# First batch of an agent-attention kernel: weights loaded between the key blocks, a later maximum, two results in one PSUM tile

## The chip, the cores and the metric

The kernel runs on one core of a Trainium2 chip. The metric is the device time of one execution in microseconds (us). Five engines work beside each other, each in its own order: TensorE (PE; its weight loads are PEld), VectorE (DVE), ScalarE (ACT), GpSimd (POOL) and SyncE (SP), which here issues every DMA.

## The reference

```python
B, N, C = (4, 12480, 128); n_agents = 49; d_ff = 2048
scale = 1.0 / np.sqrt(C)
def sm(a, b):
    s = scale * (a @ b.transpose(0, 2, 1))
    s = s - s.max(-1, keepdims=True)
    e = np.exp(s)
    return e / (e.sum(-1, keepdims=True) + 1e-09)
agent_v = sm(agents, k) @ v
x = (sm(q, agents) @ agent_v).reshape(B * N, C)
h = np.maximum(x @ w_in, 0.0)
return h * h @ w_out
```

`w_in` (128x2048) and `w_out` (2048x128) come as float64; the kernel decodes their two 32-bit words itself.

## The kernel before

**Two stages.** The first batch's attention over the keys is an opening of its own, some 80 us long, in which nothing else runs. Then a main loop goes over 52 query blocks of 960 tokens in 416 double steps; in it the other three batches' attention is spread between the products of the feed-forward network. The change touches the opening and what directly follows it.

**The opening** is written under `tc.manual_schedule()`: every engine takes its instructions in the order in which the code is written.

- `load_keys`, `load_values`: 13 key blocks (960 keys, 480 KB each) and 14 value blocks (516 KB) go through SP's queue into the tiles `ahead`, `PRE` buffers in rotation. A value block can be loaded once the block that held its buffer has been used. `load_w_in`, `load_w_out` load each weight matrix in four parts of 512 KB (tiles `raw`).
- `key(i)`: 8 matmuls give the scores of a key block for 49 agents in a PSUM bank that `bank()` hands out; ACT copies them to `s`; DVE takes a running maximum, `mx` for blocks 0 to 6 and `mx_late` for 7 to 12.
- `maximum(h)`: DVE reduces the running maximum (`m`), PE transposes it, DVE reduces again and makes a diagonal `dg`, PE spreads it over the partitions, DVE copies that to `mb`. `early` is the first half's, `late` the second's.
- `weigh(i)`: DVE subtracts the maximum, ACT takes the exponential. `gather(i)`: 8 matmuls add the weighted values of block i into PSUM (`psa` for blocks 0 to 6, `o` for 7 to 12).
- `decode_w_in`, `decode_w_out`: for each part one ACT and five DVE operations (`magnitudes`, `remainders`); for `w_in` also the sum and a maximum, for `w_out` a maximum. `powers_of_w_out` makes a power of two of the maxima (one small PE product of `e_out`), `parts_of_w_out` cuts each part into `wo_hi`, `wo_half` and `wo_lo`.
- `queries(0)`: the first query block: scores, exponential `e`, its normalisation on POOL, the split `pp`, two transposing products of `pp` on PE (below: the pp products), and small DMAs.
- `tables(0)`: the gathered sum `x` is multiplied into `w_in` in four chunks of 512 columns. `rl` is the scaled reciprocal; from it on, each chunk gets `aw_hi` (ACT), `aw_lo` and `aw_half` (DVE), and five small DMAs (`aw_hi`, `aw_ex`) that the main loop's products of that chunk wait for.

**The main loop's start.** `first(k)` multiplies a query block with one chunk into two PSUM tiles `h` (two banks each), ACT and DVE square the positive part (`r`, `gg`, `g_hi`, `g_lo`), and four slots later `second(k)` multiplies with `w_out`. Below, the double steps are called step 0, 1, 2 and so on; step 0 to 3 need chunk 0 to 3, and step 2 is the first that is followed by products with `w_out`.

**PSUM.** The pool `ps_h` has three tiles of two banks. In the kernel before, `bank()` takes a new tile for every result of the opening and uses its first bank. A tile is the unit in which the kernel's waits are kept: who writes into a tile waits until those who read what was there before are done.

Of the kernel before, what the change touches and what calls it, by code (L numbers as in the profile page):

```python
# [9 lines left out]
F32 = mybir.dt.float32  # L10
F32R = mybir.dt.float32r
# [16 lines left out]
LAG = 4  # L28
WCH = 512
WARM0 = 16  # L30
PRE = 12
HALF = 7
PAIRED = (0, 2, 4, 6, 1, 3, 5, 7)
PACE = 1.4
ONE = (NT,)
TWO = (NT // 2, NT // 2)
# [13 lines left out]
def agent_attention_relu2(ctx: ExitStack, tc: tile.TileContext, qT, kT, v, agT, w_in, w_out, outT):  # L50
# [81 lines left out]
    def decode_w_in(n, raw):  # L132
        cs = slice(n * WCH, (n + 1) * WCH)
        made = magnitudes(raw, None)
        next(made)
        t = yield from made
        yield
        low = remainders(raw, t)
        yield
        nc.vector.tensor_add(win[:, cs], t.bitcast(F32), low)  # L140
        nc.vector.reduce_max(top[:, n : n + 1], win[:, cs], axis=AX.X, apply_absolute_value=True)
# [5 lines left out]
    def decode_w_out(n, raw):  # L147
        high = raw[:, :, 1]
        nc.vector.reduce_max(most_out[:, n : n + 1], high.bitcast(F32), axis=AX.X, apply_absolute_value=True)
        yield  # L150
        made = magnitudes(raw, high)
        next(made)
        yield from made
        yield
        remainders(raw, high)
# [24 lines left out]
    def parts_of_w_out(n, raw):  # L180
        c = slice(n * WCH // C, (n + 1) * WCH // C)
        up = scale_out[0]
        t, rest = raw[:, :, 1].bitcast(F32), raw[:, :, 0].bitcast(F32)
        hi, lo, half = (x[:, c, :].rearrange("p c d -> p (c d)") for x in (wo_hi, wo_lo, wo_half))
        nc.scalar.activation(hi, t, AF.Copy, scale=up)
        nc.scalar.activation(half, t, AF.Copy, scale=up)
        yield
        nc.scalar.activation(t, t, AF.Copy, scale=up)
        nc.scalar.activation(rest, rest, AF.Copy, scale=up)
        yield  # L190
        nc.gpsimd.tensor_sub(t, t, hi.bitcast(F32))
        last[nc.gpsimd] = nc.gpsimd.tensor_add(lo, t, rest)
# [3 lines left out]

    alone = [True]

    def bank():
        if alone[0]:  # L200
            return ps_h.tile([P, 2, 512], F32, name="h")[:, 0, :]
        return ps_t.tile([P, 512], F32, name="psa", tag=f"turn{1 - turn[0]}")


# [121 lines left out]
    def tables(b):  # L326
        st = state[b]
        qd = quad.rearrange("p h a -> p (h a)")
        x = st.get("x")
        if x is None:  # L330
            x = small.tile([K2, C + 1], F32, name="x")
            nc.vector.tensor_add(x, st["av"][:, : C + 1], st["av"][:, C + 1 :])
            yield 2
        yield -1
        pa = bank()
        put([
            product(pa[:C, :K2], x[:, :C], qd, start=True, stop=True),
            product(pa[:K2, K2 : K2 + 1], qd, x[:, C:], start=True, stop=True),
        ])
        yield 1  # L340
        mag = small.tile([C, K2], F32, name="mag")
        nc.scalar.activation(mag, pa[:C, :K2], AF.Abs)
        av = small.tile([C, K2], F32, name="avT")
        nc.scalar.copy(av, pa[:C, :K2])
        rl = small.tile([K2, 1], F32, name="rl")
        nc.vector.tensor_scalar_add(rl, pa[:K2, K2 : K2 + 1], 1e-9)
        nc.vector.reciprocal(rl, rl)
        if "most" not in state:
            state["most"] = const.tile([C, 1], F32, name="most")
            nc.vector.reduce_max(state["most"], top, axis=AX.X)  # L350
        yield -1
        pu = bank()
        put([product(pu[:K2, :1], mag, state["most"], start=True, stop=True)])
        yield 1
        bound = small.tile([K2, 1], F32, name="bound")
        nc.vector.tensor_mul(bound, pu[:K2, :1], rl)
        yield -1
        ps = bank()
        put([product(ps[:, :1], ones[:K2, :], bound, start=True, stop=True)])
        yield 1  # L360
        size = small.tile([P, 1], F32, name="size")
        nc.vector.tensor_scalar(size, ps[:, :1], 2.0**-30, 2.0**60, op0=ALU.max, op1=ALU.min)
        bits = size.bitcast(U32)
        nc.vector.tensor_single_scalar(bits, bits, 0x7F800000, op=ALU.bitwise_and)
        up = small.tile([P, 1], U32, name="up")
        nc.vector.tensor_scalar(up, bits, -1.0, 280.0 * 2**23, op0=ALU.mult, op1=ALU.add)
        nc.vector.tensor_mul(rl, rl, up[:K2, :].bitcast(F32))
        st["rl"] = rl
        down = small.tile([P, 1], U32, name="down", bufs=2)
        nc.vector.tensor_scalar(down, bits, 2.0, -153.0 * 2**23, op0=ALU.mult, op1=ALU.add)  # L370
        st["down"] = down.bitcast(F32)
        nc.vector.tensor_mul(st["down"], st["down"], scale_out[1])
        hi = st["hi"] = aw.tile([P, FF], F32R, name="aw_hi")
        ex = st["lo"] = aw.tile([P, NCH // NQ, P], F16, name="aw_ex")
        yield 2
        for n in range(FF // 512):
            yield -1
            cs = slice(n * 512, (n + 1) * 512)
            pw = bank()
            put([product(pw[:K2, :], av, win[:, cs], start=True, stop=True)])  # L380
            yield 1
            last[nc.scalar] = nc.scalar.activation(hi[:K2, cs], pw[:K2, :], AF.Copy, scale=rl)
            lo = aw.tile([NA, 512], F32R, name="aw_lo")
            nc.vector.scalar_tensor_tensor(  # L384
                out=lo, in0=pw[:NA, :], scalar=rl[:NA, :], in1=hi[:NA, cs].bitcast(F32),
                op0=ALU.mult, op1=ALU.subtract,
            )
            half = aw.tile([NA, 512], F16, name="aw_half")
            nc.vector.tensor_copy(half, lo.bitcast(F32))
            yield 1  # L390
            nc.sync.dma_start(hi[K2:, cs].bitcast(F32), lo[:SP, :].bitcast(F32))
            for t in range(NQ):
                last[nc.sync] = nc.sync.dma_start(ex[t * 32 : t * 32 + NL, n, :], half[SP:, t * P : (t + 1) * P])  # L393
# [251 lines left out]
    with tc.tile_pool(name="pre", bufs=PRE) as pre, tc.manual_schedule():  # L645
# [2 lines left out]
        q0 = queries(0, pre)  # L648
        for i in range(PRE):
            kts.append(load_keys(0, i, pre, "ahead"))  # L650
            if i in (4, 7, 10):
                ins.append(load_w_in(len(ins)))

        def more(i):
            if i == 0:
                kts.append(load_keys(0, NB - 1, pre, "ahead"))
                next(q0)
                ins.append(load_w_in(len(ins)))
                return
            vts.append(load_values(0, i - 1, pre, "ahead"))  # L660
            nc.gpsimd.memset(vts[-1][:, :, C:], 1.0)
            if i - 1 in (2, 3, 5, 7):
                outs.append(load_w_out(len(outs)))

        mx = [small.tile([TP, NT, NA], F32, name=n) for n in ("mx", "mx_late")]
# [59 lines left out]
        def some(kind, n):  # L725
            if (kind, n) not in begun:
                begun[kind, n] = decode_w_in(n, ins[n]) if kind == "in" else decode_w_out(n, outs[n])
            next(begun[kind, n], None)

        for i in range(NB):  # L730
            key(i)
            more(i)
            if 6 <= i <= 8:
                next(early, None)
            if i == 10:
                weigh(0)
            if i in (3, 4, 5, 7, 8, 9, 10, 11, 12):
                some("in", (i - 3) // 4 if i < 6 else 1 if i < 10 else 2)
        ahead_of(q0, 1)
        more(NB)  # L740
        weigh(1)
        ahead_of(q0, 1)
        next(late)
        powers = powers_of_w_out()
        for i in range(NB):
            if i + 2 < NB:
                weigh(i + 2)
            gather(i)
            if i == 0:
                vts.append(load_values(0, NB - 1, pre, "ahead"))  # L750
                nc.gpsimd.memset(vts[-1][:, :, C:], 1.0)
            if i < 3:
                next(late, None)
                some("in", 3)
            if 1 <= i < NB - 2:
                ahead_of(q0, 1)
            if i == HALF + 1:
                nc.vector.tensor_scalar_mul(x[:NA, :], sums[0][:NA, : C + 1], fall)
            if 3 <= i < NB - 1:
                some("out", (i - 3) // 3)  # L760
            if i == NB - 3:
                some("out", 3)
                next(powers)
            if i == NB - 2:
                run(powers)
        run(q0)
        ahead = queries(1)
        next(ahead)
        cut = [parts_of_w_out(n, outs[n]) for n in range(NW)]
        next(cut[0])  # L770
        next(cut[0])
        spun.append(ps_t.tile([P, 512], F32, name="psa", tag="turn1"))
        spin(2)
        nc.vector.tensor_add(x[:NA, :], x[:NA, :], sums[1][:NA, : C + 1])
        for at, _ in enumerate(tables(0)):
            if at in (1, 3):
                spin(2)
            if at == 2:
                next(cut[1])
        spin(5)  # L780
        seen = small.tile([K2, 1], F32, name="seen")
        nc.gpsimd.tensor_copy(seen, st["rl"])
        run(cut[0])
        some("out", 3)
        some("out", 3)
        for gen in cut[1:]:
            run(gen)
    behind = [last[eng].ins for eng in (nc.sync, nc.scalar, nc.gpsimd)]

# [107 lines left out]
```

## Time and profile before

| | us |
|---|---|
| median of 3 runs (1893.69 to 1894.61) | 1894.58 |
| the profiled execution's own time | 1894.66 |
| its span, first to last instruction | 1892.9 |
| first gather starts | 40.18 |
| first pp product starts | 54.74 |
| `rl` of the tables is scaled, ends | 77.25 |
| step 3 starts, PE without gaps from here | 101.40 |

All times below count from the span's start. The stages follow each other on PE: key blocks, gathers, tables, the first steps of the main loop. From about 101 us to the end PE works without a break that matters, so the length of the opening is read from when PE reaches given instructions. "Granted clock" 1.00 is 2.4 GHz, 0.50 is 1.2 GHz.

### The profile page before, as it was taken

The page shows a single profiled execution, that of the slowest core. Times are in us where ns is not written, and L with a number is a line of the kernel's source. Part 1 is how long each engine was busy: PE and PEld are TensorE (multiplying, and loading weights), DVE is VectorE, ACT ScalarE, POOL GpSimd, SP SyncE. Part 2 cuts the span into 40 slices and gives each one's busy share as a digit, 9 for nine tenths or more (in the row PEclk, how much of TensorE's full clock was granted, in tenths as well). Part 3 has the DMA queues.
Part 4 walks back from the last instruction along what each step waited for, and adds up shares of the span by engine and source line. Part 5 has one row for each costly group of instructions (what it writes and reads, how often), then busy time and mean ns, then how long its engine had stood idle before and what let it go on. Part 6 is the DMA issues. An engine that isn't in the chain of part 4 may idle for free.

```text
span 1892.9 us, 31062 instructions
## 1 busy us (share of the span) xinstructions
PE 1875.7 (99%) x10851; PEld 1426.4 (75%) x10851; DVE 1644.1 (87%) x1870; ACT 1670.0 (88%) x1587; POOL 1326.6 (70%) x1269
## 2 busy tenths in 40 slices
PE   9899999999999999999999999999999999999999
PEld 9677777777777777777777777777777777777776
DVE  5787888888998898888898888888889989899997
ACT  2587899999888899999888889999988999999997
POOL 0255688887666678888766668889866676767675
PEclk7899999999999999999999999999999999999999
DMA  9143222222122222222211212222111111111110
GB/s 366 51 133 105 70 84 95 84 92 83 48 66 71 78 70 83 92 87 90 74 55 60 85 51 66 89 74 75 62 41 56 51 53 52 51 53 44 55 37 28
DMA packets 73780, 145.06 MB, mean 77 GB/s; under 512 B 9244, under 2 KB 45752, under 8 KB 73624
## 3 DMA queue, kind: packets, MB, share of 16 engines
q1 hardware_dynamic: 73624, 143.07, 23.7%
q8 instruction: 86, 1.41, 0.3%
q14 instruction: 70, 0.57, 0.1%
HBM read 83.42 MB, written 25.56 MB: 58 GB/s over the span
## 4 chain that ended last, share of the span: by engine, by line
PE 94%; DVE 3%; ACT 1%; issue 1%; DMA 0%; POOL 0%; SPq 0%; POOLq 0%; ACTq 0%; DVEq 0%
PE o L490 56%; PE h L490 25%; PE psa L490 10%; PE h L674 1%; DVE gg L490 1%; ACT r L490 1%; ACT g_hi L490 0%; DMA ahead<-in_v 0%; PE h L639 0%; PE psa L715 0%; DVE g_lo L490 0%; PE h L224 0%; DVE ob L490 0%; POOL g_lo L521 0%; SPq L393 0%
## 5 line engine op out<-in xcount | busy, mean ns | idle before, releaser
L521 POOL TENSOR_TENSOR g_lo<-gg,g_hi 128x480 f16<-128x480 f32 x832 | 998.3, 1222 | 451.5 <-ACT g_hi L490 256.4
L490 ACT ACTIVATE r<-h 128x960 f32<-128x960 f32 x832 | 763.6, 968 | 125.5 <-PE h L490 98.4
L490 ACT ACTIVATE g_hi<-r 128x1920 fp32r<-128x1920 f32 x416 | 755.0, 1815 | 26.8 <-ACT r L490 0.4
L490 DVE TENSOR_TENSOR g_lo<-h,g_hi 128x960 f16<-128x960 f32 x416 | 480.2, 1154 | 121.3 <-ACT g_hi L490 94.1
L490 PE MATMUL o<-g_hi,wo_hi 128*128 128x480 f32 x1664 | 571.0, 424 | 0.0
L490 DVE TENSOR_TENSOR gg<-r,h 128x960 f32<-128x960 f32 x416 | 478.9, 1151 | 80.6 <-ACT r L490 71.5
L490 PE MATMUL o<-g_lo,wo_half 128*128 128x480 f16 x1664 | 516.6, 370 | 0.7 <-POOL g_lo L521 0.5
L490 PE MATMUL o<-g_hi,wo_lo 128*128 128x480 f32 x1664 | 498.7, 381 | 0.0
L490 DVE TENSOR_TENSOR h<-r,h 128x960 f32<-128x960 f32 x416 | 480.3, 1155 | 0.7
L490 PE MATMUL h<-w,aw_hi 128*128 128x480 f32 x1664 | 433.2, 381 | 5.0 <-DVE aw_lo L384 2.0
L490 PEld LDWEIGHTS h<-w,aw_hi 128*128 128x128 f32 x1664 | 310.3, 188 | 61.1 <-DVE gg L490 8.1
L490 PEld LDWEIGHTS o<-g_hi,wo_hi 128*128 128x128 f32 x1664 | 315.2, 189 | 50.8 <-issue 3.7
L490 PEld LDWEIGHTS o<-g_hi,wo_lo 128*128 128x128 f32 x1664 | 312.7, 188 | 50.5
L490 PEld LDWEIGHTS <-wo_half 128*128 128x128 f16 x1664 | 167.3, 115 | 124.9 <-issue 92.2
L490 PE MATMUL h<-x,aw_ex 19*128 19x480 f16 x1664 | 159.7, 372 | 0.5 <-DMA aw_ex<-aw_half 0.5
L490 PEld LDWEIGHTS psa<-ag,qt 128*120 128x120 f32 x816 | 140.2, 186 | 18.8 <-DVE ob L490 4.4
L490 PE MATMUL psa<-ag,qt 128*120 128x49 f32 x816 | 126.1, 242 | 0.0
L490 PEld LDWEIGHTS <-aw_ex 19*128 19x128 f16 x1664 | 41.9, 91 | 107.3 <-issue 99.9
L490 PEld LDWEIGHTS psa<-ag,kt 128*120 128x120 f32 x624 | 93.5, 184 | 8.6 <-DVE ob L490 0.5
L490 PE MATMUL psa<-ag,kt 128*120 128x49 f32 x624 | 87.6, 249 | 0.0
L307 POOL TENSOR_TENSOR vs<-vt,vs 120x1024 fp32r<-120x1024 f32 x39 | 86.0, 2206 | 0.0
L490 DVE TENSOR_SCALAR ob<-o,down 128x480 f32<-128x480 f32 x104 | 72.4, 696 | 4.0 <-PE o L490 4.0
(165 smaller groups left out, 1046.8 us busy)
## 6 DMA issues: line engine op xcount, KB each, us to landing
qt<-in_qT SPq DMA_DIRECT2D x52, 480.0 KB
out_T<-ob SPq DMA_DIRECT2D x104, 240.0 KB
vt<-in_v SPq DMA_DIRECT2D x39, 516.0 KB
kt<-in_kT SPq DMA_DIRECT2D x39, 480.0 KB
w<-ph SPq DMA_DIRECT2D x102, 91.9 KB
w<-y SPq DMA_DIRECT2D x102, 91.9 KB
x<-half SPq DMA_DIRECT2D x416, 17.8 KB
ahead<-in_v SPq DMA_DIRECT2D x14, 516.0 KB
```

The costliest lines, as they stand in the source:

```text
L307: nc.gpsimd.tensor_sub(vs[:, :, C + 1 : 2 * C + 1], vt[:, :, :C], vs[:, :, :C].bitcast(F32))
L490: ins = issue(*args, **kw)
L521: chain[nc.gpsimd] = nc.gpsimd.tensor_sub(lo[:, n, :], gg[:, n, :], hi[:, 0, n, :].bitcast(F32)).ins
L674: nc.tensor.matmul(sv[:, t, :], kts[i][:, t * TP : (t + 1) * TP], ag[:, 0, :], start=True, stop=True)
```

## The change

- The loads: `PRE` goes from 12 to 11. The four parts of `w_in` are loaded after key blocks 1, 3, 6 and 9, the four of `w_out` after the first four value blocks.
- The decode is spread by two tables: which part takes its next piece after which key block (`BESIDE_KEYS`) and after which gather (`BESIDE_VALUES`). The ACT operation of a part now stands a piece ahead of its DVE operations.
- `early` advances after key blocks 6, 8 and 9 instead of 6, 7 and 8; `weigh(0)` to `weigh(2)` stand behind key blocks 10 to 12.
- `bank()` hands out both banks of a tile, one after the other: two successive results share one tile `h`. In the opening these are key blocks 0 and 1, 2 and 3, 4 and 5, 6 and 7, then block 8 with the transposed maximum, 9 with the spread one, 10 and 11, 12 with the query scores.
- `most`, the maximum of `w_in`, is taken before the gathers. The powers of `w_out` are taken at gathers 6 and 8, and the parts are cut at gathers 9 to 12 and in the tables. Parts 2 and 3 get `wo_lo` from two DVE operations instead of two on ACT and two on POOL.
- `aw_lo` has three buffers and `aw_half` four, instead of two each.

```diff
-PRE = 12
+PRE = 11
+BESIDE_KEYS = ((0, 0), (0, 1), (1,), (1,), (1,), (2, 2), (), (2,), (2, 3), (3,), (3,), (), ())
+BESIDE_VALUES = ((), (), (0,), (1, 0), (2, 0), (3, 0), (1,), (1, 1), (2,), (2, 2), (3,), (3,), ())
...
         nc.scalar.activation(half, t, AF.Copy, scale=up)
         yield
+        if n > 1:
+            for out, x, y, op in ((t, t, hi.bitcast(F32), ALU.subtract), (lo, rest, t, ALU.add)):
+                nc.vector.scalar_tensor_tensor(out=out, in0=x, scalar=up, in1=y, op0=ALU.mult, op1=op)
+            return
...
+    spare = []
+
     def bank():
         if alone[0]:
-            return ps_h.tile([P, 2, 512], F32, name="h")[:, 0, :]
+            if not spare:
+                h = ps_h.tile([P, 2, 512], F32, name="h")
+                spare.extend((h[:, 1, :], h[:, 0, :]))
+            return spare.pop()
...
-            lo = aw.tile([NA, 512], F32R, name="aw_lo")
+            lo = aw.tile([NA, 512], F32R, name="aw_lo", bufs=3)
...
-            half = aw.tile([NA, 512], F16, name="aw_half")
+            half = aw.tile([NA, 512], F16, name="aw_half", bufs=4)
...
-            if i in (4, 7, 10):
+            if i in (1, 3, 6, 9):
                 ins.append(load_w_in(len(ins)))
...
-            if i - 1 in (2, 3, 5, 7):
+            if i - 1 < NW:
                 outs.append(load_w_out(len(outs)))
...
+        some("in", 0)
         for i in range(NB):
             key(i)
             more(i)
-            if 6 <= i <= 8:
+            if i in (6, 8, 9):
                 next(early, None)
-            if i == 10:
-                weigh(0)
-            if i in (3, 4, 5, 7, 8, 9, 10, 11, 12):
-                some("in", (i - 3) // 4 if i < 6 else 1 if i < 10 else 2)
+            for n in BESIDE_KEYS[i]:
+                some("in", n)
+            if i > 9:
+                weigh(i - 10)
...
-            if 3 <= i < NB - 1:
-                some("out", (i - 3) // 3)
-            if i == NB - 3:
-                some("out", 3)
-                next(powers)
-            if i == NB - 2:
-                run(powers)
+            for n in BESIDE_VALUES[i]:
+                some("out", n)
+            if i in (6, 8):
+                next(powers, None)
+            if i == 7:
+                cut = [parts_of_w_out(n, outs[n]) for n in range(NW)]
+            if i > 8:
+                next(cut[(i - 9) // 2])
...
             if at == 2:
-                next(cut[1])
+                next(cut[2])
+            if at == 9:
+                next(cut[3])
+                some("out", 3)
+            if at == 11:
+                run(cut[2])
```

On TensorE, the key blocks of the kernel before, each in a PSUM tile of its own (the number behind `h` is the tile):

```order
L674 MATMUL h_169<-ag_82,ahead_130 120x49 x8
L674 MATMUL h_186<-ag_82,ahead_132 120x49 x8
L674 MATMUL h_201<-ag_82,ahead_134 120x49 x8
L674 MATMUL h_216<-ag_82,ahead_136 120x49 x8
L674 MATMUL h_238<-ag_82,ahead_138 120x49 x8
```

The same place in the changed kernel, on TensorE:

```order
L683 MATMUL h_171<-ag_82,ahead_130 120x49 x8
L683 MATMUL h_171<-ag_82,ahead_132 120x49 x8
L683 MATMUL h_214<-ag_82,ahead_136 120x49 x8
L683 MATMUL h_214<-ag_82,ahead_138 120x49 x8
L683 MATMUL h_253<-ag_82,ahead_142 120x49 x8
L683 MATMUL h_253<-ag_82,ahead_144 120x49 x8
L683 MATMUL h_291<-ag_82,ahead_146 120x49 x8
L683 MATMUL h_291<-ag_82,ahead_150 120x49 x8
L683 MATMUL h_324<-ag_82,ahead_152 120x49 x8
L698 MATMUL h_324<-ident_86,m1_306 49x120
```

Two blocks now stand in one tile, and the built program gives the second of each pair a wait for the readers of the first: block 1 waits for ACT's copy of block 0, blocks 3, 5, 7 and 11 for DVE's maximum of the block before, the transposed maximum for that of block 8, the spread one for that of block 9, and the query scores for that of block 12.

On VectorE, the readers of these tiles in the changed kernel and what stands between them (`t`, `rest`, `raw`, `win` and `top` are the decode of `w_in`):

```order
L691 TENSOR_TENSOR mx_160<-s_180,h_171 120x392
L143 TENSOR_TENSOR win_101<-t_169,raw_134 128x512
L144 TENSOR_REDUCE top_102<-win_101 128x1
L691 TENSOR_TENSOR mx_160<-mx_160,h_214 120x392
L112 TENSOR_SCALAR t_212<-t_212 128x512
L115 TENSOR_SCALAR t_212<-t_212 128x512
L117 SCALAR_TENSOR_TENSOR t_212<-raw_140,t_212 128x512
L691 TENSOR_TENSOR mx_160<-mx_160,h_214 120x392
L124 TENSOR_SCALAR rest_250<-t_212 128x512
L126 SCALAR_TENSOR_TENSOR raw_140<-raw_140,rest_250 128x512
L691 TENSOR_TENSOR mx_160<-mx_160,h_253 120x392
```

The decode of part 0 now stands among the maxima of blocks 1 to 4; in the kernel before it began behind that of block 3.

On VectorE, at the tables, the changed kernel between the first two chunks (`aw_lo_714` and `aw_lo_732`):

```order
L394 SCALAR_TENSOR_TENSOR aw_lo_714<-h_711,rl_688,aw_hi_709 49x512
L399 CAST aw_half_716<-aw_lo_714 49x512
L124 TENSOR_SCALAR rest_720<-raw_268 128x512
L126 SCALAR_TENSOR_TENSOR raw_268<-raw_268,rest_720 128x512
L194 SCALAR_TENSOR_TENSOR raw_248<-raw_248,up_out_609,wo_hi_103 128x512
L194 SCALAR_TENSOR_TENSOR wo_lo_104<-raw_248,up_out_609 128x512
L394 SCALAR_TENSOR_TENSOR aw_lo_732<-h_711,rl_688,aw_hi_709 49x512
```

Four operations on `w_out` have moved in between; before, the second `aw_lo` followed the first `aw_half`.

## Rows read from the trace of the kernel before

**Rows 1.** The page's part 2: granted clock in 40 equal slices, tenths of full speed.

```profile
PEclk7899999999999999999999999999999999999999
```

**Rows 2.** Stretches: length, busy time and count by engine, granted clock, DMA share, GB/s.

```profile
8.00:20.00 12.00, 12.00 (x117) 12.00 (x116) 6.67 (x13) 3.97 (x8) 0.00 (x0) 1.00 1.03 410
23.00:24.00 1.00, 1.00 (x5) 0.83 (x4) 0.70 (x2) 0.45 (x1) 0.00 (x0) 0.50 1.02 408
43.00:44.00 1.00, 1.00 (x7) 0.68 (x6) 0.07 (x1) 0.77 (x2) 0.00 (x0) 0.84 1.06 401
72.00:74.00 2.00, 2.00 (x10) 1.62 (x9) 0.28 (x1) 1.96 (x3) 0.00 (x0) 0.50 0.06 22
84.00:86.00 2.00, 0.28 (x1) 0.00 (x0) 1.34 (x2) 2.00 (x3) 0.53 (x1) 0.57 0.15 37
101.00:102.00 1.00, 1.00 (x5) 0.87 (x4) 0.60 (x4) 0.92 (x1) 0.00 (x1) 0.83 0.76 281
```

**Rows 3.** Timeline of TensorE: start, duration, instruction, count, idle time before and releaser.

```profile
6.93 13.54 PE L674 MATMUL h<-ag,ahead 128*120 128x49 f32 x128
21.28 0.28 PE L689 MATMUL h<-ident,m 120*49 120x120 f32 x1 [0.81 <-DVE m L686]
...
24.01 13.04 PE L674 MATMUL h<-ag,ahead 128*120 128x49 f32 x64
...
40.18 3.48 PE L715 MATMUL psa<-ahead,s 120*49 120x129 f32 x16
...
43.82 1.97 PE L715 MATMUL psa<-ahead,s 120*49 120x129 f32 x16
...
46.06 7.59 PE L715 MATMUL psa<-ahead,s 120*49 120x129 f32 x64
54.74 0.56 PE L224 MATMUL h<-identr,pp 120*98 120x120 f32 x4 [1.09 <-POOL pp L295]
...
61.56 5.52 PE L715 MATMUL o<-ahead,s 120*49 120x129 f32 x48
69.68 0.38 PE L170 MATMUL h<-e_out,ones 128*128 128x1 f32 x2 [2.61 <-DVE e_out L165]
```

**Rows 4.** Timelines of ScalarE and VectorE: a key block's copy and maximum, a decode operation.

```profile
8.75 0.48 ACT L676 COPY s<-h 120x392 f32<-120x392 f32 x1 [6.42 <-PE h L674]
12.62 0.56 DVE L682 TENSOR_TENSOR mx<-mx,h 120x392 f32<-120x392 f32 x1 [1.12 <-ACT s L676]
18.41 0.68 DVE L140 TENSOR_TENSOR win<-t,raw 128x512 f32<-128x512 f32 x1
```

**Rows 5.** The chain of waits, and GpSimd's timeline, ahead of the first pp product.

```profile
45.86 6.15 DMA ahead<-in_v
...
52.27 0.85 POOL e L424
53.74 0.95 POOL L295 TENSOR_TENSOR pp<-e,pp 120x392 fp32r<-120x392 f32 x1 [0.63 <-ACT pp L293]
```

**Rows 6.** Timelines of VectorE and ScalarE: decode of `w_out`, its parts, the tables.

```profile
54.68 0.43 DVE L110 TENSOR_SCALAR t<-t 128x512 f32<-128x512 f32 x1 [2.56 <-ACT t L108]
57.15 0.70 DVE L124 SCALAR_TENSOR_TENSOR raw<-raw,rest 128x512 f32<-128x512 uint32 x1
71.17 0.75 ACT L185 ACTIVATE wo_hi<-raw,up_out 128x512 fp32r<-128x512 f32 x1 [4.55 <-DVE up_out L175]
74.54 0.25 ACT L342 ACTIVATE mag<-h 128x98 f32<-128x98 f32 x1 [0.56 <-PE h L224]
77.09 0.16 DVE L367 TENSOR_TENSOR rl<-rl,up 98x1 f32<-98x1 f32 x1
```

**Rows 7.** Timelines of VectorE and TensorE at the main loop's first steps.

```profile
80.08 0.73 DVE L384 SCALAR_TENSOR_TENSOR aw_lo<-h,rl,aw_hi 49x512 fp32r<-49x512 f32 x1
86.27 2.23 PE L490 MATMUL h<-w,aw_hi 128*128 128x480 f32 x4 [1.99 <-DVE aw_lo L384]
93.69 1.14 PE L490 MATMUL h<-w,aw_hi 128*128 128x480 f32 x2 [1.30 <-issue]
101.40 1.04 PE L490 MATMUL h<-w,aw_hi 128*128 128x480 f32 x4
```

More of the change, by code (lines that the diff above doesn't have):

```diff
@@ L135, in decode_w_in @@
         next(made)
+        yield
         t = yield from made
@@ L152, in decode_w_out @@
         next(made)
+        yield
         yield from made
@@ L347, in tables @@
         nc.vector.reciprocal(rl, rl)
-        if "most" not in state:
-            state["most"] = const.tile([C, 1], F32, name="most")
-            nc.vector.reduce_max(state["most"], top, axis=AX.X)
         yield -1
@@ L655, in more @@
             if i == 0:
-                kts.append(load_keys(0, NB - 1, pre, "ahead"))
+                kts.extend(load_keys(0, n, pre, "ahead") for n in range(PRE, NB))
                 next(q0)
-                ins.append(load_w_in(len(ins)))
                 return
@@ L732, in agent_attention_relu2 @@
             more(i)
-            if 6 <= i <= 8:
+            if i in (6, 8, 9):
                 next(early, None)
-            if i == 10:
-                weigh(0)
-            if i in (3, 4, 5, 7, 8, 9, 10, 11, 12):
-                some("in", (i - 3) // 4 if i < 6 else 1 if i < 10 else 2)
+            for n in BESIDE_KEYS[i]:
+                some("in", n)
+            if i > 9:
+                weigh(i - 10)
         ahead_of(q0, 1)
         more(NB)
-        weigh(1)
+        next(late)
+        some("in", 3)
+        state["most"] = const.tile([C, 1], F32, name="most")
+        nc.vector.reduce_max(state["most"], top, axis=AX.X)
         ahead_of(q0, 1)
-        next(late)
         powers = powers_of_w_out()
         for i in range(NB):
-            if i + 2 < NB:
-                weigh(i + 2)
+            if i + 3 < NB:
+                weigh(i + 3)
             gather(i)
@@ L753, in agent_attention_relu2 @@
                 next(late, None)
-                some("in", 3)
             if 1 <= i < NB - 2:
@@ L768, in agent_attention_relu2 @@
         next(ahead)
-        cut = [parts_of_w_out(n, outs[n]) for n in range(NW)]
-        next(cut[0])
-        next(cut[0])
         spun.append(ps_t.tile([P, 512], F32, name="psa", tag="turn1"))
@@ L782, in agent_attention_relu2 @@
         nc.gpsimd.tensor_copy(seen, st["rl"])
[L783 to L786, printed above, removed]
+        for gen in cut:
             run(gen)
```

## The prediction

> **What bounds the kernel now.** I read the granted clock first. All of the half clock lies in the first two of 40 slices [rows 1], in the opening, and the stretches say where: full speed from 8 to 20 us, half at 23 to 24, back during 43 to 44, half again at 72 to 74, partly at 84 to 86, and full for good during 101 to 102 [rows 2]. So the change, which touches no more than the opening and the first steps, can be priced by when PE reaches four marks: first gather, first pp product, scaled `rl`, step 3.
>
> The timeline of TensorE gives what stands between them [rows 3]. 128 records in 13.54 us are eight key blocks (a matmul has two records, a block 16): 1.69 us each at full clock. 64 in 13.04 are four blocks: 3.26 each at half clock. The blocks follow each other without idle time, since each has its own tile; keys come in at 410 GB/s beside them [rows 2]. So **key phase and gathers are bound by PE and its clock**. The first pp product waits for GpSimd [rows 3], and the chain leads from there to a value load that lands at 45.86 + 6.15 = 52.01 [rows 5]. Later PE waits 2.61 us for `e_out` [rows 3], then the clock is at half [rows 2].
>
> The median, 1894.58, is 0.08 below the profiled execution's 1894.66 with a span of 1892.9; I add differences of marks to 1894.66.
>
> **The change, part by part.**
>
> *First mark, start of the first gather, 40.18 before.* The loads move, but a half-clock PE needs 3.26 us a block where key and weight parts together need some 20 us for all 8.3 MB at 410 GB/s, so they cost nothing while PE is slow. What costs is the shared PSUM tile: the second block of a pair now waits until the first has been read. Block 0 takes no wait; it ends about 8.73 as before, its copy runs from 8.75 for 0.48 [rows 4], and block 1 ends near 11.2, block 2 near 12.9. The copy of block 2 ends near 13.4, VectorE has `win` of the decode ahead (0.68) and then the maximum of 0.56 [rows 4], so block 3 starts near 14.25 and ends near 16.05. A hold is copy 0.48 + maximum 0.56 + three handovers of 0.02 to 0.14, 1.22 together. Such holds stand ahead of blocks 5, 7, 11, of the two products of the early maximum, and of the query scores: six more.
>
> The dear part is what the holds do to the clock. Before, an idle time of 0.81 us ahead of the early maximum's product at 21.28 [rows 3] is followed by half clock at 23 to 24 [rows 2]. Against that, the 1.09 us ahead of 54.74 did not lower it: the gathers behind take 5.52/3 = 1.84 us [rows 3], full speed. One hold may thus pass and a row of them hardly will; I take the fall after the second long hold, at about 16 us. Then ten blocks (4 to 12 and the query scores) at 3.2 are 32.0, six holds 7.3, weight loads that the holds uncover 1.3 (estimate: 0.2 each), the early maximum's two products 0.8: 16.05 + 41.4 = **57.4, +17.2**. Ends: a fall at the first hold, at 11 us, adds 3.0 (two blocks at 1.57 more); a fall only at about 22 us takes 4.7 off; no fall at all gives 41.6 (ten times 1.57 less).
>
> *Second mark, first pp product, 14.56 after the first gather before (54.74 − 40.18).* GpSimd's product `e` waits behind the clearing of the buffer of the last value block's load, and with `PRE` = 11 the last three loads wait for gathers 0, 1 and 2. Three gathers at full speed are 1.9 + 0.16 + 1.97 + 0.27 + 1.9 = 6.2 [rows 3]. The clock returns some way into them: before it took 3.1 us (40.18 to about 43.3, from 0.84 granted at 43 to 44 [rows 2]), a loss of 1.55; at the steps 6.3 us or more (behind 93.69's two products, to about 101.3 [rows 2, 7]), a loss of 3.15; I take 2.4. The load then lies between 1.3 us (516 KB at 401 GB/s [rows 2]) and the 6.15 it took among others [rows 5]; it is the last one in flight, so nearer the lower: 3.3. From landing to pp product it was 2.73: `e` 0.85, `pp` 0.95 and what lies between [rows 5]. Sum 14.6, **+0.1**, first pp product at 72.1. PE's own six gathers take 14.4, no later. Ends: −2.7 (smaller loss 0.8, load 1.9 less) and +3.7 (larger loss 0.8, load 2.9 more).
>
> *Third mark, `rl` scaled, 22.5 later before (77.25).* The 2.61 us wait for `e_out` [rows 3] goes, since the powers are taken at gathers 6 and 8; with it goes the half clock that follows (70.6 to 74, some 1.2 us of work lost; [rows 2] shows 72 to 74), and `most` leaves the chain (0.5, estimate). That would be 18.2. But VectorE and ScalarE now end later. Behind the first pp product VectorE has two decodes of five operations (3 × 0.43 + 2 × 0.70 = 2.7 each [rows 6]), four subtractions of 0.56's size [rows 4] and some eight small ones of 0.16 to 0.43 [rows 6]: +10.0. Then ScalarE: last exponential 0.45, a cast 0.6, `wo_hi` and `wo_half` of part 0 at 0.75 [rows 6], another 0.6, then six full-width operations of 0.68 [rows 4] that stand ahead of `mag` on the two engines: +17.1 for `mag`. From `mag` to scaled `rl` it was 77.25 − 74.54 = 2.7 [rows 6], less `most`'s 0.5: 19.3, **−3.2**. Ends: −4.3 (the waits alone) and −2.0 (two operations of 0.68 more ahead of `mag`).
>
> *Fourth mark, step 3, 24.15 after `rl` before (101.40 − 77.25).* Between the first two `aw_lo` VectorE now has four operations of 128x512, 0.43 + 3 × 0.70 = 2.5 [rows 6]: the second `aw_lo`, which ended at 80.81 = `rl` + 3.56 [rows 7], ends at + 6 to + 7.3, and behind it waits the chunk's DMA, and behind that step 1 (86.27 = + 9.0 before [rows 7]), now about + 12. Step 2 stood at 93.69, + 16.4, with 1.30 idle [rows 7] and VectorE then busy with the rest of a decode, which has gone from there. Step 1's products and query scores, about 5.9 at half clock, put step 2 at + 17.9; to step 3 it is then 7.7 (93.69 to 101.40 at half [rows 7]) or 3.9 at full; with a clock that comes back 3.1 to 6.8 us on, + 23.3 to + 25.6. I take 24.5, **+0.3**; bounds −3.8 (clock never down) and +1.5. Sum: 17.2 + 0.1 − 3.2 + 0.3 = +14.4, **1909**.
>
> **The rivals.**
>
> *A, the clock holds (not slower).* If holds of 1.2 us don't lower the clock, the first gather starts at 41.6; the first pp product is then set by the load, about 54.4 (−0.3); the third and fourth terms stay: −3.2 in all, 1891.5. For it: 1.09 us ahead of 54.74 left the clock up [rows 3]. Against: 0.81 us did not [rows 2, 3], and here six or more follow each other, one every 4.7 us. The point where it decides is the number of blocks at half clock: four of them make it +4.5, one still gives about zero. The Trainium skill, "TensorE: Matmul & The Clock Gate", section "🎯 Why this matters for your kernels", warns of idle gaps between bursts that are longer than any hold here; by that rule the clock would stay and A would hold. The trace does not agree with it: the fall behind the 0.81 us.
>
> *B, the halves don't hold each other.* If the two banks of a tile were independent, keys would end as PE allows: no holds, the key phase at full clock, gathers from about 31.4, but the first pp product still bound by the last value load, at about 54.1 (a little earlier than before, as loads start earlier), then −3.2 + 0.3: 1891.2. Against it: the built program has the waits. The Trainium skill, "PSUM — Partial Sum Buffer", section "🎯 Summary: rules for kernel authors", advises a different bank for reading while a matmul runs; by it the pairs could overlap and B would hold. No run here shows that, and the waits are kept by tile.
>
> *C, the clock falls at the first hold* and returns late in the gathers: +3.0 and +1: 1913.
>
> *D, the clock falls late*, at block 5 to 9: five to eight blocks at half clock, 1.57 each less than the ten: 1899 to 1905.
>
> **How the numbers follow.** Forecast (fall at about 16 us, 1905 to 1911) 0.58; A 0.12; B 0.03; C 0.12; D 0.15. Likeliest 1909. The range takes the forecast, C with its unknown load (to 1914) and D but for its end, from 1900: a little over 0.8. About 0.2%, 3.8 us, is what a measurement here tells from no change: 1890.8 to 1898.4. A and B lie in that, at its lower end; a little more gain in the third mark makes them faster: 0.05 faster, 0.10 within, 0.85 slower.
>
> **What would show it.** In the changed kernel's profile TensorE should have idle times of 1.1 to 1.4 us, released by VectorE's `mx`, ahead of blocks 3, 5, 7, 11 and the query scores; granted clock 0.50 from about 16 to 60 us; four key blocks in 13 us there; first gather at 57 ± 3; first pp product near 72 behind GpSimd's `pp`; no 2.6 us wait for `e_out`; `rl` scaled near 91.5; step 3 near 116, and from there the same rows as before, 14 us later. I am wrong if the blocks between the holds take 1.7 us (A), if there are no holds (B), if the first pp product does not follow the third gather's load (second mark), or if `mag` waits for PE and not for ScalarE (third mark).

## The result, and the profile after

The changed kernel takes 1909.18 us (median, 1907.02 to 1909.75) where the kernel before takes 1894.53, measured beside it: a ratio of 1.0076, interval 1.0059 to 1.0094. It is slower by 14.65 us. The profiled execution is the shortest of the four, 1907.02 with a span of 1905.2; its marks are compared below with those of the profiled execution before.

| mark | before | after | difference of the stretch | predicted |
|---|---|---|---|---|
| first gather starts | 40.18 | 57.02 | +16.84 | +17.2 |
| first pp product starts | 54.74 | 71.77 | +0.19 | +0.1 |
| scaled `rl` ends | 77.25 | 90.98 | −3.30 | −3.2 |
| step 3 starts | 101.40 | 112.05 | −3.08 | +0.3 |
| end of the span | 1892.89 | 1905.19 | +1.65 | 0 |

The timeline of TensorE after (start, duration, instruction, count, idle time before and its releaser) answers to [rows 3]:

```profile
9.42 3.56 PE L683 MATMUL h<-ag,ahead 128*120 128x49 f32 x32 [0.57 <-ACT s L685]
14.26 4.83 PE L683 MATMUL h<-ag,ahead 128*120 128x49 f32 x32 [1.28 <-DVE mx L691]
20.27 6.63 PE L683 MATMUL h<-ag,ahead 128*120 128x49 f32 x32 [1.17 <-DVE mx L691]
...
35.97 0.41 PE L698 MATMUL h<-ident,m 120*49 120x120 f32 x1 [1.26 <-DVE mx_late L691]
...
53.65 3.44 PE L237 MATMUL h<-ag,qt 128*120 128x49 f32 x16 [1.17 <-DVE mx_late L691]
57.02 3.68 PE L724 MATMUL psa<-ahead,s 120*49 120x129 f32 x16
...
71.77 0.56 PE L237 MATMUL h<-identr,pp 120*98 120x120 f32 x4 [1.39 <-POOL pp L308]
...
104.33 1.43 PE L500 MATMUL h<-w,aw_hi 128*128 128x480 f32 x4
...
107.71 1.53 PE L500 MATMUL h<-w,aw_hi 128*128 128x480 f32 x4
...
112.05 1.33 PE L500 MATMUL h<-w,aw_hi 128*128 128x480 f32 x4
```

(The last three are the starts of step 1, 2 and 3.) The scaled `rl` on VectorE:

```profile
90.82 0.16 DVE L377 TENSOR_TENSOR rl<-rl,up 98x1 f32<-98x1 f32 x1
```

Every second block waits for the reader of the first of its pair, and 32 records (two blocks) take 3.56 us at the beginning and 6.63 later. The granted clock over the same time (stretch, length, busy time of PE, PEld, DVE, ACT, POOL, granted clock, DMA share, GB/s) falls at about 16.3 and is back at about 60.7:

```profile
16.00:18.00 2.00, 2.00 (x14) 2.00 (x13) 1.27 (x3) 0.49 (x1) 0.00 (x0) 0.57 1.05 414
...
60.00:62.00 2.00, 2.00 (x15) 1.52 (x14) 0.96 (x4) 0.00 (x0) 0.00 (x0) 0.83 0.15 15
```

(A stretch of 2 us at 0.57 has 0.14 of its length at full clock, so the fall is at 16.3. All points of a fall below are read in this way.)

How much of the 16.84 us is waiting and how much is slow work is in the groups of the key phase, TensorE alone, shapes apart (busy time, mean ns of one, idle time before). First the changed kernel from 6 to 57 us:

```profile
L683 PE MATMUL h<-ag,ahead 128*120 128x49 f32 x208 | 36.8, 358 | 5.4 <-DVE mx L691 3.6 <-DVE mx_late L691 1.2 <-ACT s L685 0.6
L706 PE MATMUL h<-dg,ones 49*120 49x49 f32 x2 | 0.6, 414 | 1.2 <-DVE mx_late L691 1.2
```

then the kernel before, from 6 to 41 us:

```profile
L674 PE MATMUL h<-ag,ahead 128*120 128x49 f32 x208 | 28.7, 310 | 0.0
```

The eight holds are 0.57 + 1.28 + 1.26 + 5 × 1.17 = 8.96 us (the 5.4 and 1.2 of the groups, and the 1.26 and 1.17 ahead of 35.97 and 53.65), against 0.81 of idle time before [rows 3]: +8.15. The same 208 records take 36.8 us instead of 28.7, since more of them run at half clock: +8.1. These two are about 16.3 of the 16.84.

### The profile page after: what moved, and what is told of

Read it like the earlier page. It is cut to its first block, busy times and chain, and to the rows that moved or that the text cites. A ratio compares the mean times of both kernels' runs of the same rounds, so it can differ in the third digit from the quotient of the medians.

```text
span 1905.2 us, 31045 instructions
## 1 busy us (share of the span) xinstructions
PE 1879.0 (99%) x10851; PEld 1430.5 (75%) x10851; DVE 1647.6 (86%) x1874; ACT 1668.1 (88%) x1583; POOL 1323.2 (69%) x1265
## 4 chain that ended last, share of the span: by engine, by line
PE 93%; DVE 3%; ACT 2%; issue 1%; POOL 0%; DMA 0%; POOLq 0%; DVEq 0%; ACTq 0%; SPq 0%
PE o L500 56%; PE h L500 25%; PE psa L500 10%; PE h L683 2%; DVE gg L500 1%; ACT r L500 0%; PE psa L724 0%; POOL g_lo L531 0%; DVE h L500 0%; PE h L649 0%; DVE g_lo L500 0%; ACT g_hi L500 0%; PE h L237 0%; ACT s L685 0%; DMA ahead<-in_v 0%
```

## Experiments

The prediction has two causes in the first mark: the shared tile holds blocks, and the holds bring the clock down. The first six kernels take them apart.

**own_tiles**: the changed kernel without sharing.

```diff
-            if not spare:
-                h = ps_h.tile([P, 2, 512], F32, name="h")
-                spare.extend((h[:, 1, :], h[:, 0, :]))
-            return spare.pop()
+            return ps_h.tile([P, 2, 512], F32, name="h")[:, 0, :]
```

> The changed kernel, but every result of the opening takes a PSUM tile of its own again, as before. Theory (the shared tiles hold the key blocks, and the holds lower the clock): no idle time ahead of key blocks 3, 5, 7 and 11, blocks of 1.7 us, first gather at 31 to 34 us instead of 57.0, first pp product at 47 to 54, then 19 us to the scaled `rl` and 21 to 23 more to step 3: 1882 to 1892 us. Rival (the new places of the loads and of the decode make the key phase slow, the tiles don't matter): first gather stays above 50, 1904 to 1909.

Measured: 1893.27 us, ratio to before 0.9991 (0.9981 to 1.0000). The sharing alone is thus worth 15.9 us (1909.18 − 1893.27), all of the loss; the rest of the change is not told from zero. The time is 1.3 us above the theory's range, and the first gather at 44.68 was not early. The profiled execution took 1896.43 us, 3.2 above the median, at a mean granted clock of 0.986 where seven of the ten have 0.989 to 0.991; in those the clock may have fallen later, which no trace shows. The group of the key blocks, the timeline of TensorE and two stretches of the key phase:

```profile
L680 PE MATMUL h<-ag,ahead 128*120 128x49 f32 x208 | 34.5, 348 | 0.0
```

```profile
6.55 21.39 PE L680 MATMUL h<-ag,ahead 128*120 128x49 f32 x144
...
44.68 3.68 PE L721 MATMUL psa<-ahead,s 120*49 120x129 f32 x16
```

```profile
13.00:14.00 1.00, 0.98 (x10) 0.89 (x10) 1.00 (x3) 0.59 (x2) 0.00 (x0) 1.00 1.01 415
...
15.00:16.00 1.00, 1.00 (x9) 1.00 (x8) 1.00 (x3) 0.49 (x1) 0.00 (x0) 0.61 1.03 415
```

No hold is left, and yet the clock falls, at 15.2 us: long holds are not needed for it. What there is ahead of the fall is one small break, between 13 and 14 us, where PE is busy for 0.98 and its weight loads for 0.89 of the stretch.

**shared_before**: the kernel before with the sharing alone (the diff above the other way round).

> The kernel before with one part of the change: two successive results share a PSUM tile. Theory: holds of about 1.2 us ahead of every second block, half clock from the third or fourth pair on, first gather at 54 to 59 us instead of 40.2, and since the later stages stay as before, 1907 to 1913. Rival (sharing alone costs nothing, it takes the new decode order on VectorE): within 3 us of 1894.6.

Measured: 1913.74 us, ratio 1.0095 (1.0080 to 1.0110); 39.0 us of busy key blocks and holds of 1.17 us:

```profile
14.13 6.63 PE L679 MATMUL h<-ag,ahead 128*120 128x49 f32 x32 [1.17 <-DVE mx L687]
...
57.45 3.27 PE L720 MATMUL psa<-ahead,s 120*49 120x129 f32 x16
```

```profile
12.00:14.00 2.00, 0.96 (x8) 0.79 (x6) 0.66 (x2) 0.49 (x1) 0.00 (x0) 0.59 1.02 415
```

The theory's mechanism holds (the time is 0.7 us above its range), and the rival that blames the new order on VectorE falls: with the old order the first gather is at 57.45. Here the clock fell sooner than expected, at 12.4, after the first hold.

**spins**: the changed kernel with its holds filled.

```diff
         for i in range(NB):
             key(i)
+            if i in (0, 2, 4, 6, 8, 9, 10, 12):
+                spin(3)
```

> The changed kernel with the holds left in, and three products of ones (0.35 us each at full clock) put on TensorE into each of the eight holds of the opening, into a bank that nothing else uses there. Theory (two thirds of the loss is the clock that falls behind the idle times): the clock stays at full, blocks take 1.7 us, first gather at 41 to 44 us, first pp product at 54 to 57, 1890 to 1896. Rival (the holds themselves are the loss, or the clock falls for another reason): half clock from about 16 us as in the changed kernel, first gather at 56 to 60, 1907 to 1911.

Measured: 1902.19 us, ratio 1.0042 (1.0029 to 1.0055), between theory and rival. Filling the first 0.9 us of each hold left idle times of 0.44 to 0.85 us, and the clock stayed up for ten microseconds longer, to 26.2:

```profile
14.26 3.56 PE L683 MATMUL h<-ag,ahead 128*120 128x49 f32 x32 [0.55 <-DVE mx L691]
...
51.45 3.68 PE L724 MATMUL psa<-ahead,s 120*49 120x129 f32 x16
```

```profile
26.00:28.00 2.00, 2.00 (x14) 2.00 (x12) 0.00 (x0) 0.49 (x1) 0.00 (x0) 0.55 1.06 366
```

Work on TensorE that is of no use makes the kernel 7.0 us shorter: the clock's part of the loss is real and hangs on what TensorE does in the holds. The other 8.9 us, to own_tiles, are close to the length of the holds, which stay in; but the clock still fell, at 26.2, so this split is an estimate.

**before_again** and **after_again**: both kernels unchanged, a second profiled execution each, to see whether the fall lies at the same place in another execution.

> The kernel before, looked at a second time. Theory (the clock falls in the key blocks of its own, at another point in each execution): the fall is not at 22.8 us again but anywhere from 12 to 28, and the first gather moves with it, 1.57 us for each key block, between 36 and 46. Rival (the fall is set by the idle time of 0.81 us ahead of the early maximum's product): fall at 22 to 23 us, first gather at 40.2 within 0.5.

> The changed kernel, looked at a second time. Theory: holds of 1.17 to 1.28 us in the same eight places, the fall at another point, 11 to 20 us, the first gather at 54 to 61. Rival (the holds set the fall): fall at 16.3 within 1 us, first gather at 57.0 within 1.

Measured: 1894.68 and 1907.19 us. The first gather is at 40.18 again and at 57.01, and the clock falls again at 22.7 and 16.3:

```profile
22.00:24.00 2.00, 2.00 (x14) 1.83 (x13) 1.61 (x4) 0.44 (x1) 0.00 (x0) 0.68 1.05 420
```

```profile
16.00:18.00 2.00, 2.00 (x14) 2.00 (x13) 1.28 (x3) 0.49 (x1) 0.00 (x0) 0.57 1.02 407
```

So neither kernel gave a sign of the fall that wanders, my theory, and the rival is nearer. But two executions of each do not settle it: in low_as_before, below, the changed kernel's key phase is at half clock from 14.0. The gathers of the kernel before did go another way the second time. TensorE waited 1.93 us ahead of the first pp product instead of 1.09, and half clock followed from 56.8 to 60.3.

**six**: every result of the opening in a tile of one bank, six in rotation, so that no block waits for a reader.

```diff
-    ps_h = ctx.enter_context(tc.tile_pool(name="ps_h", bufs=3, space=PSUM))
...
-            return spare.pop()
+            return banks[0].tile([P, 512], F32, name="h")
...
+    with tc.tile_pool(name="ps_0", bufs=6, space=PSUM) as ps_0, tc.tile_pool(name="pre", bufs=PRE) as pre, tc.manual_schedule():
+        banks.append(ps_0)
...
+    ps_h = ctx.enter_context(tc.tile_pool(name="ps_h", bufs=3, space=PSUM))
```

> The changed kernel with the six banks of the opening as six tiles of one bank each, so that neither the pairs hold each other (as in the changed kernel) nor a fourth block waits for VectorE (as with three tiles; there the key blocks paused 0.2 us at 13.2 us and the clock was at half from 15.2). Theory 1 (any pause on TensorE tips the clock): no pause, full clock to the end of the key blocks, first gather at 30 to 35 us, 1879 to 1888. Theory 2 (key blocks in a row cannot keep the clock, pause or not): half clock from some point between 12 and 26 us, first gather at 38 to 46, 1888 to 1896.

Measured: 1895.82 us, ratio 1.0006 (0.9997 to 1.0015). The time lies in the range of theory 2, and the first gather, 36.08, in neither. In the key blocks theory 1 is nearer: nine blocks run without a break at full clock, and the fall comes at 26.4, behind the small products of the early maximum at 22.3 and 24.35:

```profile
7.00 15.24 PE L680 MATMUL h<-ag,ahead 128*120 128x49 f32 x144
22.29 0.28 PE L695 MATMUL h<-ident,m 120*49 120x120 f32 x1
...
36.08 3.68 PE L721 MATMUL psa<-ahead,s 120*49 120x129 f32 x16
...
55.21 0.92 PE L233 MATMUL h<-identr,pp 120*98 120x120 f32 x4 [5.63 <-POOL pp L304]
...
84.97 1.97 PE L496 MATMUL h<-w,aw_hi 128*128 128x480 f32 x4 [6.30 <-DVE aw_lo L390]
```

```profile
26.00:28.00 2.00, 2.00 (x15) 2.00 (x13) 1.93 (x5) 0.48 (x1) 0.00 (x0) 0.60 1.08 367
```

The first gather is 21 us sooner than in the changed kernel, but TensorE then waits 5.63 us for GpSimd and 6.30 at step 0. In the changed kernel the waits at these two places are 1.39 and 3.26; most of the remaining kernels are about them.

With all fourteen profiles the breaks can be set against the falls. "First break" is the first place where TensorE does not go straight from one key block's product to the next. The kernels that have not come yet are described below; the profiled executions of own_tiles, six_13 and keys6 were among the longest of their kernels.

| kernel | first break, us | what it is | clock falls |
|---|---|---|---|
| before, twice | 20.5 and 20.4 | 0.81, early maximum | 22.8 and 22.7 |
| own_tiles | 13.2 | under 0.2, a small break | 15.2 |
| keys6 | 13.0 | about 0.2, a small break | 14.7 |
| six | 22.3 | early maximum's product | 26.4 |
| six_13_low | 22.4 | early maximum's product | 27.2 |
| six_13 | 16.6 | 0.21, a key load | 18.4 |
| best2 | 16.8 | 0.23, a key load | 18.7 |
| best1 | 18.3 | 0.64, a key load | 21.6 |
| shared_before | 8.6 | 0.57, hold | 12.4 |
| changed kernel, twice | 8.8, then 13.0 | 0.57 and 1.28, holds | 16.3 |
| low_as_before | 9.4, then 13.5 | 0.58 and 1.28, holds | 14.0 |
| spins | 13.7, 18.5, 23.3 | 0.55, 0.44, 0.85, rests of filled holds | 26.2 |

In none of the fourteen profiles did a fall come ahead of the first break. The holds come earlier than any other break, but not each fall that follows them does: with a break of 0.2 us alone, own_tiles and keys6 were at half clock sooner (15.2 and 14.7) than the changed kernel (16.3). Not every break is followed by a fall: the first hold of the changed kernel was not, the shortened holds of spins at 13.7 and 18.5 us were not, and the 1.09 us ahead of 54.74, among the gathers [rows 3], were not either. The length of a break was not varied by itself, so this is a pattern of the profiles and no rule that was tested.

**low_as_before**: the changed kernel with parts 2 and 3 of `w_out` cut as before.

```diff
-        if n > 1:
-            for out, x, y, op in ((t, t, hi.bitcast(F32), ALU.subtract), (lo, rest, t, ALU.add)):
-                nc.vector.scalar_tensor_tensor(out=out, in0=x, scalar=up, in1=y, op0=ALU.mult, op1=op)
-            return
```

> The changed kernel, but parts 2 and 3 of `w_out` get their low parts from two ScalarE and two GpSimd operations again, so two full-width operations less stand between the first two `aw_lo` on VectorE. Theory: the idle time of 3.26 us ahead of the second half of step 0 falls to about 1.8, step 3 comes 1 to 2 us sooner than 112.05, the opening to the scaled `rl` stays: 1905 to 1908. Rival (ScalarE, which limits the way to `mag`, is made longer, or the second `aw_lo` is not what step 0 waits for): 1909 to 1912.

Measured: 1907.25 us, ratio 1.0062 (1.0047 to 1.0077). The interval overlaps that of the changed kernel, so the 1.9 us are not settled by the times; the rows say more. In the changed kernel VectorE, between the first two `aw_lo`:

```profile
91.92 0.74 DVE L394 SCALAR_TENSOR_TENSOR aw_lo<-h,rl,aw_hi 49x512 fp32r<-49x512 f32 x1 [0.68 <-ACT aw_hi L392]
...
93.80 1.51 DVE L124 TENSOR_SCALAR rest<-raw 128x512 uint32<-128x512 uint32 x1
95.34 1.42 DVE L126 SCALAR_TENSOR_TENSOR raw<-raw,rest 128x512 f32<-128x512 uint32 x1
96.67 0.74 DVE L194 SCALAR_TENSOR_TENSOR raw<-raw,up_out,wo_hi 128x512 f32<-128x512 f32 x1
97.45 0.75 DVE L194 SCALAR_TENSOR_TENSOR wo_lo<-raw,up_out 128x512 fp32r<-128x512 f32 x1
98.12 0.74 DVE L394 SCALAR_TENSOR_TENSOR aw_lo<-h,rl,aw_hi 49x512 fp32r<-49x512 f32 x1
```

and TensorE at the second half of step 0, first in the changed kernel, then in this one:

```profile
98.91 1.17 PE L500 MATMUL h<-w,aw_hi 128*128 128x480 f32 x2 [3.26 <-DVE aw_lo L394]
```

```profile
97.26 0.70 PE L496 MATMUL h<-w,aw_hi 128*128 128x480 f32 x2 [0.25 <-DVE aw_lo L390]
```

The wait of 3.26 us is VectorE's work between the two `aw_lo`, but the two operations that have gone are only 1.5 us of it. The two that stay take 1.1 us here where they took 2.9:

```profile
94.40 0.41 DVE L124 TENSOR_SCALAR rest<-raw 128x512 uint32<-128x512 uint32 x1
94.84 0.69 DVE L126 SCALAR_TENSOR_TENSOR raw<-raw,rest 128x512 f32<-128x512 uint32 x1
```

GpSimd worked beside them in the changed kernel (1.92 of every 2 us from 92 to 96) and started only at 95.28 here. From the scaled `rl` to step 3 it is 18.86 us, 21.07 in the changed kernel. The scaled `rl` itself comes 1.4 us later. Up to the last gathers the edit changes nothing, and yet the clock is at half already from 14.0 and the first gather is at 59.36:

```profile
14.00:16.00 2.00, 1.20 (x6) 1.20 (x7) 1.93 (x5) 0.04 (x1) 0.00 (x0) 0.50 1.02 409
```

So the place of the fall differs between executions of the same key phase.

**six_13**: as six, without the fourteenth value load.

```diff
-            if i == 0:
-                vts.append(load_values(0, NB - 1, pre, "ahead"))
-                nc.gpsimd.memset(vts[-1][:, :, C:], 1.0)
```

> As the six single-bank tiles, and the fourteenth value load (block 12 a second time, which nothing reads) with its clearing on GpSimd left out. Theory (the first pp product waits for that load): the pause of about 1.1 us ahead of the first pp product goes, nothing else changes: 0.5 to 2 us below the kernel with six tiles. Rival (the load before it lands no sooner): same within 0.5.

**six_13_low**: and with low_as_before's edit.

> As the six single-bank tiles without the fourteenth load, and the low parts 2 and 3 on ScalarE and GpSimd as before. Theory (the two VectorE operations between the first two `aw_lo` cost 2 us from the scaled `rl` to step 3, as with the changed kernel's 21.07 against 18.86): 1 to 3 us below the kernel without them. Rival: same within 0.5.

Measured: 1892.98 us, ratio 0.9991 (0.9981 to 1.0001), and 1891.18, ratio 0.9982 (0.9972 to 0.9991). The medians give 2.8 us for the load, somewhat more than expected, and 1.8 for the low parts, as expected; the intervals of neighbours overlap, and only the two edits together, 4.6 us against six, are clear of it. But the wait ahead of the first pp product has not gone. It does not show in six_13, whose clock fell sooner and whose first gather came at 42.7; in six_13_low, where it came at 35.5, TensorE waits 4.10 us, because the load before the one left out is now the one that GpSimd waits for (its clearing, and `e` directly behind it at 51.23):

```profile
51.11 0.11 POOL L663 MEMSET ahead<- 120x8 f32 x1 [1.22 <-DMA ahead<-in_v]
```

**keys6**: six tiles up to the pp products, and the changed kernel's pairs from the tables on.

```diff
         run(q0)
+        opening.__exit__(None, None, None)
+        banks.clear()
+        ps_h = ctx.enter_context(tc.tile_pool(name="ps_h", bufs=3, space=PSUM))
         ahead = queries(1)
```

> The changed kernel, with six tiles of one bank each up to the first query block's products, and the pairs kept from the tables on. Theory (the pairs cost in the key blocks and gain at the tables, where with six single tiles the first step waited 6.30 us for the last `aw_lo` since its two banks lay under the tables' results): no holds, first gather at 35 to 45 us, step 0 at scaled `rl` + 4 instead of + 10.2, step 3 at + 19 to + 22 instead of + 25.3: 1889 to 1893. Rival (step 0 waits for something else): as the kernel with six tiles throughout, 1894.0 to 1897.6.

Measured: 1898.07 us, ratio 1.0011 (1.0002 to 1.0021), above both ranges and no better than six. The pairs were not those of the changed kernel: there the transposed `x` is the second of a pair, here the first, so that the second chunk shares a tile with the third, and waits are again the result:

```profile
87.37 3.73 PE L238 MATMUL h<-win,avT 128*98 128x512 f32 x4 [4.98 <-DVE aw_lo L395]
```

**best1**: keys6 with six_13's and low_as_before's edits, and with the clearings of value blocks 5 to 12 moved on GpSimd behind the first query block's products `e` and `pp`.

```diff
-            nc.gpsimd.memset(vts[-1][:, :, C:], 1.0)
+            if i < 6:
+                nc.gpsimd.memset(vts[-1][:, :, C:], 1.0)
...
+            if i == 4:
+                for vt in vts[5:]:
+                    nc.gpsimd.memset(vt[:, :, C:], 1.0)
```

**best2**: best1 with one bank left out ahead of the tables, which restores the changed kernel's pairs there.

```diff
         ps_h = ctx.enter_context(tc.tile_pool(name="ps_h", bufs=3, space=PSUM))
+        bank()
```

> As the kernel with six tiles for the keys and pairs at the tables, with three more edits: no fourteenth value load, the clearings of the later value buffers stand on GpSimd behind the first query block's normalisation and split, and low parts 2 and 3 of `w_out` on ScalarE and GpSimd as before. Theory (the first pp product waits on GpSimd for clearings that wait for value loads, which left TensorE idle for 4.1 to 5.6 us): no such idle time, first pp product about 14.5 us after the first gather, then 17 to 20 us to the scaled `rl` and 19 to 22 to step 3: 1880 to 1888. Rival (VectorE and ScalarE set the end of the opening, so the time returns ahead of `mag`): 1888 to 1892.

> As the kernel best1, but one bank is left out at the tables, so that the four chunks share tiles in the pairs of the changed kernel (first with second, third with fourth) and not second with third. Theory (which results share a tile at the tables decides when PE comes back to dense work: 18.9 us from the scaled `rl` to step 3 in the changed kernel with the old low parts, 26.1 with the other pairs): step 3 at the scaled `rl` + 18 to + 21, clock at half there for 3.4 to 7 us instead of 17: 1882 to 1888. Rival (the steps start late for another reason): as best1, 1890 to 1893.

Measured: 1891.72 us, ratio 0.9979 (0.9970 to 0.9989), and **1886.02 us, ratio 0.9950 (0.9936 to 0.9963)**: the second is faster than both kernels. The wait ahead of the first pp product is gone in both (best1: 14.25 us behind the first gather), but best1 lost it again at the tables. The chunk that waits, step 0 and step 3 on TensorE, best1:

```profile
76.94 3.73 PE L234 MATMUL h<-win,avT 128*98 128x512 f32 x4 [3.85 <-DVE aw_lo L391]
...
82.46 1.40 PE L497 MATMUL h<-w,aw_hi 128*128 128x480 f32 x4
...
97.72 1.02 PE L497 MATMUL h<-w,aw_hi 128*128 128x480 f32 x4
```

and best2:

```profile
75.23 1.96 PE L234 MATMUL h<-win,avT 128*98 128x512 f32 x4 [1.56 <-DVE aw_lo L391]
...
77.55 0.68 PE L497 MATMUL h<-w,aw_hi 128*128 128x480 f32 x2 [0.36 <-DMA aw_hi<-aw_lo]
...
91.81 1.32 PE L497 MATMUL h<-w,aw_hi 128*128 128x480 f32 x4
```

One unused bank changes which results share a tile, and with it the way from the scaled `rl` to step 3: 26.07 us in best1, 18.31 in best2. What is left in best2's key phase is the break at a key load (its row in the table). That the weights loaded between the key blocks make that load late is likely but not shown: no kernel moved them back by themselves.

## Why the prediction was right

**First mark: right in size, right on the holds, too simple on the clock.** +16.84 against +17.2. The holds were priced at 1.22 us, measured 1.17 to 1.28 (0.57 at the copy), and the fall taken at about 16 us came at 16.3. The prediction took the fall for a consequence of repeated holds of 1.2 us, but only one of them stood ahead of it (the next began at 19.1). own_tiles and six show that a break of 0.2 us, or the early maximum's products alone, are followed by a fall too, and low_as_before has it at 14.0 in the same key phase. So that the point came out at 16 is in part luck, and what sets it stays open. Nor is all of the slow work the holds' doing: without them the key blocks took 34.5 us in own_tiles' profile and 25.4 in that of six, against 36.8 with them and 28.7 before. The 0.2 us that each hold was to cost in uncovered weight loads stands in no row; two blocks between holds took 6.63 us where half of [rows 3]'s four is 6.52, so it was about 0.1. Rival A, a clock that stays up, is refuted by the fall at 16.3; the idle times did not have to be long for it. (Rival D's own terms, two to five blocks fewer at 1.57 us, give 1901 to 1906, not 1899 to 1905.)

**Rival B is refuted** for these programs: the built program's waits are the holds, and where each result has its own tile (own_tiles, six) they are gone.

**Second mark: right, for the reasons given.** The third gather ends at 65.1, and the last value load takes over (GpSimd's `e` follows at 69.30):

```profile
65.14 3.90 DMA ahead<-in_v
```

3.9 us against the 3.3 taken, the half-clock loss smaller by about as much; from landing (69.04) to the product at 71.77 it is 2.73 as in [rows 5].

**Third mark: right.** The 2.61 us wait of [rows 3] has gone, and `mag` comes late from ScalarE, as the sum said. ScalarE's timeline, where it stands behind six operations of 0.73 to 0.76 us in a row, and TensorE's wait:

```profile
88.77 0.23 ACT L355 ACTIVATE mag<-h 128x98 f32<-128x98 f32 x1
```

```profile
89.05 0.33 PE L237 MATMUL h<-most,mag 128*98 128x1 f32 x2 [1.19 <-ACT mag L355]
```

17.0 us from the first pp product to `mag`, 17.1 predicted.

**Fourth mark: mis-sized by 3.4 us.** The second `aw_lo` started at `rl` + 7.1 and ended at + 7.9 (predicted + 6 to + 7.3), since the four operations ahead of it took 4.3 us (93.80 to 98.12) and not 2.5, and step 1 came at + 13.35 (+ 12). The step that failed is what comes behind: the prediction let step 1's products and the query scores run at half clock and step 2 start at + 17.9; it started at + 16.7. The clock was at half only from 98.2 to 105.0, where before it had been so from 84.3 to 101.3 [rows 2]:

```profile
98.00:100.00 2.00, 1.09 (x2) 0.50 (x2) 1.93 (x4) 0.00 (x0) 0.00 (x0) 0.55 0.00 0
...
104.00:106.00 2.00, 2.00 (x12) 1.37 (x10) 1.97 (x4) 0.97 (x1) 0.95 (x1) 0.74 0.11 26
```

From 98.91 TensorE works without a pause that the timeline shows (step 0's second half, the last chunk, the products of ones), and the clock is back 0.7 us into step 1; step 1 to step 3 takes 7.7 us instead of 15.1. The prediction had the clock back 3.1 to 6.8 us into dense work (the 6.8 stands in no row); it was 6.1, but counted from step 0 and not from step 2. The wait was counted as a delay only; that the work behind it then stands in one piece, early enough for the clock to be back at step 1, was not.

**The rest of the span, +1.65, was not foreseen.** 0.6 of it is idle time ahead of two transposing products in a step that follows (0.82 us at 120.29 instead of 0.20 at 108.74, both for VectorE's `mx`); the rest comes in smaller steps.

So the agreement of 1909.18 with 1909 is in part luck. In the profiled execution the five differences make +12.3, not +14.4: the fourth mark is 3.4 us below its term and the rest 1.65 above. That the median came out right is due to the other three executions, which are 2.1 to 2.7 us longer at a mean granted clock of 0.984 instead of 0.986, and both profiles are of the shorter kind (1907.02 and 1907.19). Where the longer ones stay at half clock was not seen, and that is open.

## What to carry to other kernels

A tile is the unit of waiting: two results in the banks of one tile are no longer double buffering, and every second producer waits for the readers of the first. Ask of each change to the buffers which instruction waits for which reader in the built program, and price the wait together with what the engine's clock does behind it. The same sharing can help later: from the scaled `rl` to step 3 it was 21.07 us with the pairs, 23.04 with a tile for each result (own_tiles), 25.28 with six small tiles and 28.80 with the pairs shifted by one result (keys6). So choose it stage by stage.

## What the runs showed of the hardware that was not expected

In a row of key blocks, 1.69 us each, TensorE kept full clock for fifteen microseconds as long as nothing broke the row (six: 7.0 to 22.3), and a break of 0.2 us was followed by half clock 2 us later (own_tiles, keys6, six_13, best2). It did not come back in the key blocks in any profile; it came back 2 to 6 us into the gathers each time (before 43.3, changed kernel 60.7, own_tiles 49.4).

On VectorE, `rest` and `raw` took 1.51 and 1.42 us at 93.80 and 95.34 in the changed kernel, where GpSimd was busy for 1.92 of every 2 us from 92 to 96, and 0.41 and 0.69 in low_as_before at 94.40 and 94.84, where GpSimd was idle until 95.28: the same operations, two to four times as long. In six, with GpSimd as busy (76 to 80), they took 1.51 and 1.42 again.
